# Numerators of the attention on 32x32 tiles: eight token tiles at once in place of four, a smaller DMA scratch for GpSimd, and a new order of the parts

## The chip, the cores and the metric

The kernel runs on one core of a Trainium2 chip. The metric is the time of one execution on the device in microseconds, the median of several runs. The engines are TensorE (PE, with PEld for its weight loads), VectorE (DVE), ScalarE (ACT), GpSimd (POOL) and SyncE (SP), whose queue issues the DMAs.

## The reference, cut to what matters

2048 tokens of width 512, in f32. Branch A is linear attention with 32 heads of width 16, whose feature map is a pair of softmaxes per head; branch B is dense, Mish, dense; the output is x + A * silu(B).

```python
xn = _layernorm(x, axis=-1)
# A: per head, with q, k, v = parts of xn @ wqkv
phi_q = concat([softmax(q @ w_phi), softmax(-q @ w_phi)], -1)      # the same for phi_k
kv  = einsum("bhsf,bhsd->bhfd", phi_k, v)
z   = einsum("bhsf->bhf", phi_k)
num = einsum("bhqf,bhfd->bhqd", phi_q, kv)
den = einsum("bhqf,bhf->bhq", phi_q, z)[..., None] + 1e-6
s   = (num / den) @ wo
# B
h = xn @ w1 + b1
g = silu((h * tanh(softplus(h))) @ w2)
return x + s * g
```

The change is about num, the product of a token's 32 features of a head with that head's 32x16 matrix kv.

## The kernel before

The 2048 tokens are 16 tiles of 128. Nearly every large product is made of three fp32r matmuls on the parts hi and lo of its operands (mm3). The program is a list of parts, named in ORDER (line 36). N normalizes and transposes a tile of x; K, V and Q project a tile (K and Q with the softmaxes); A adds a pair of tiles to kv; z makes the sums; D (den, line 604) multiplies a Q tile by the reciprocal of its denominators and lets VectorE transpose it into a buffer; Ua and Ub (lines 639 and 642) are the two halves of the numerators of a group of tiles; O (att_out, line 655) applies wo and stores the tile in DRAM; L, P, M and R load and prepare for the FFN; Fa to Fd (fx, fz, fy) are its first product, G (y) its second; E is the end of a group of four tiles: silu, product with the stored attention, sum with x.

The order of TensorE is that of ORDER, word for word. For the other engines and SyncE's DMAs a planner (simulate, line 177) makes the order at build time: it goes through the program with estimated costs, gives each free engine the ready operation with the earliest due time, which comes from the place in ORDER of the TensorE part that needs it, and chooses the engine where two can do the operation (either, copy). The result is fixed. At run time each engine works its list in order and waits on semaphores.

A numerator half works on 32x32 tiles of TensorE. A tile is a row group b (32 partitions, which after VectorE's transposes of 32x32 blocks hold a head's 32 features of the tokens 32b to 32b + 31 of each token tile) and a column group m; 16 tiles exist at a time. For each of 4 b, 4 m, 2 s and 2 c there is one matmul with a stationary 32x32 piece of kv and 128 moving columns: 64 matmuls for a half, 128 for a group of four token tiles, two halves each for four groups. Each is f32, and the trace shows two records for it:

```python
PE.matmul(pn[b][32 * m:32 * m + 32, c, :], w["kv"][at, h % 4, h // 4 * 32:h // 4 * 32 + 32],
          ph[at, h].rearrange("p j n -> p (j n)"), start=s == 0, stop=s == 1, skip_group_check=True)
```

The moving operand is the transposed Q of a group (ph, from a pool of one buffer of 16 KB a partition, tag tq). The four results pn (one bank of PSUM each, of eight) are kept over both halves; after the second, 8 pairs of operations on ScalarE and VectorE (split, line 429) copy them out as hi and lo parts oh and ol, in four tiles from the pool "slot". The pool's 38 buffers of 4 KB also hold weights, FFN operands and prefetched loads.

Of the kernel before, what the change touches and what calls it, by code (L numbers as in the profile page):

```python
# [12 lines left out]
F32R = mybir.dt.float32r  # L13
# [19 lines left out]
SLOTS, S2 = 38, 11  # L33
SLACK, AHEAD, LAT = 15000, 40000, 150
WAKE = 13
ORDER = """
wk0 N0 wv0 b1 wq0 N1 N2 P3 wk1 K0 N4 N8 K1 wv1 V1 K2 V0 V2 N5 K4 N3 K8 V3 K3 wq1 N6 N7 K5 A0 V4 V5 N9 A1 N10 K9 K6 K7
V6 N12 P2 A2 V7 V8 P0 V9 L0 Fa3 K10 N11 A3 A4 V11 K11 Fa0 V12 K12 V10 Fb0 Fc0 N13 Fb3 Fc3 Q5 Fd3 P1 Fd0 N14 N15 A5 V15
K13 V14 K14 K15 V13 Fa1 Fb1 Fc1 P6 Fa6 M2 Fa2 A6 A7 Fb6 Fc6 Fd1 Q4 P4 Fa4 Q0 Fd6 Fb2 z D0 D4 P5 Fa5 Q1 Fb5 Fc5 Q8 Fb4
Fc4 Fd5 M4 Fc2 Fd4 Fd2 L1 Fa9 Fb9 Q2 D1 Fa11 Fb11 Fc11 M1 Q6 Fc9 Fd11 Fd9 D5 M6 Fa13 D6 D2 Q3 Fb13 Fc13 D3 Fa8 Fb8 Fc8  # L40
Fd13 Q10 Q14 Fd8 M0 Fa7 Fb7 Q9 Fc7 D8 Ua0 D9 Q7 Fd7 Ub0 M5 Fa12 wo1 Fb12 Fc12 Q11 Fd12 D7 Q15 Q12 M3 Fa10 Fb10 Fc10
wo0 O0 O1 R2 Fd10 Ua1 R5 O3 O2 R4 R0 G7 R1 G8 Ub1 G9 O7 R3 Q13 G0 G1 G2 G3 R6 G4 G5 G6 D10 O6 O5 G10 G11 G12 G13 E0 O4
E1 G14 D11 D12 D13 Ua2 G15 Ub2 G16 G17 G18 G19 G20 D14 D15 Ua3 O10 O11 O9 Ub3 G21 G22 O14 O15 O8 E2 O13 O12 G23 G24
G25 G26 E3
"""
ACT_SET = {AF.Exp: 1, AF.Silu: 3, AF.Mish: 2}

# [5 lines left out]
class Program:  # L53
# [317 lines left out]
def block_kernel(ctx: ExitStack, tc: tile.TileContext, x, wqkT, wv, phi, wo, w1, b1, w2, out):  # L371
    nc = tc.nc
    prog = Program(nc)
    PE, V, G, A, Q = (Engine(prog, e) for e in ("PE", "V", "G", "A", "Q"))
# [3 lines left out]
    psum = ctx.enter_context(tc.tile_pool(name="psum", bufs=8, space=bass.MemoryType.PSUM))  # L378
    dram = ctx.enter_context(tc.tile_pool(name="dram", bufs=1, space=bass.MemoryType.DRAM))
    pools = {}  # L380
    for tag, n in (("slot", SLOTS), ("s2", S2), ("sm", 13), ("rq", 5), ("st", 3 * NT), ("tq", 1)):
        pools[tag] = ctx.enter_context(tc.tile_pool(name=tag, bufs=n))
        prog.cap[tag] = n
    prog.cap["ps"] = 8
# [2 lines left out]
    def bank(shape, name):  # L387
        t = psum.tile(shape, F32, tag="ps", name=name)
        prog.tag[t.tensor.name] = "ps"
        return t  # L390

    def alloc(tag, shape, name, dtype=F32):
        t = pools[tag].tile(shape, dtype, tag=tag, name=name)
        prog.tag[t.tensor.name] = tag
        return t

    def slot(shape, name, dtype=F32):
        return alloc("slot", shape, name, dtype)
# [171 lines left out]
    ek, eq, rq, phT, oT = {}, {}, {}, {}, {}  # L570
# [33 lines left out]
    def den(t):  # L604
        ez = slot([P, H, 2, DH], f"ez{t}")
        either(ez, eq[t], w["z"], op=ALU.mult)
        tz = sm([P, 2 * H], f"tz{t}")
        V.tensor_reduce(tz, ez.rearrange("p h s d -> p (h s) d"), axis=X, op=ALU.add)
        r = rq.pop(t)
        dn = sm([P, H], f"den{t}")  # L610
        V.tensor_tensor(tz, tz, r, op=ALU.mult)
        tz3 = tz.rearrange("p (h s) -> p h s", s=2)
        V.scalar_tensor_tensor(dn, tz3[:, :, 0], 1e-6, tz3[:, :, 1], op0=ALU.add, op1=ALU.add)
        V.reciprocal(dn, dn)
        r3 = r.rearrange("p (h s) -> p h s", s=2)
        V.tensor_tensor(r3, r3, dn[:, :, None].to_broadcast([P, H, 2]), op=ALU.mult)
        scale(eq[t], r)

        g, j = divmod(t, 4)
        if g not in phT:  # L620
            phT[g] = alloc("tq", [P, H, 4, 32], f"ph{g}")
        V.transpose(phT[g][:, :, j, :], eq[t].rearrange("p h s d -> p h (s d)"))

    pns = {}

    def num_half(g, i):
        ph, pn = phT[g], pns[g]
        with one():
            for c in (2 * i, 2 * i + 1):
                for s in range(2):  # L630
                    for m in range(4):
                        h = 8 * c + 2 * m + s
                        for b in range(4):
                            at = slice(32 * b, 32 * b + 32)
                            PE.matmul(pn[b][32 * m:32 * m + 32, c, :], w["kv"][at, h % 4, h // 4 * 32:h // 4 * 32 + 32],
                                      ph[at, h].rearrange("p j n -> p (j n)"), start=s == 0, stop=s == 1, skip_group_check=True)
            prog.halves()

    def num_a(g):
        pns[g] = [bank([P, KC, P], f"pn{g}_{b}") for b in range(4)]  # L640
        num_half(g, 0)

    def num_b(g):
        num_half(g, 1)
        pn = pns.pop(g)
        for u in (2 * g, 2 * g + 1):
            oT[u] = slot([P, KC, 2, P], f"oh{u}", F32R), slot([P, KC, 2, P], f"ol{u}", F32R)
        for b in range(4):
            for u in range(2):
                src = pn[b].rearrange("p k (j n) -> p k j n", j=4)[:, :, 2 * u:2 * u + 2]  # L650
                split(src, *(o[:, :, :, 32 * b:32 * b + 32] for o in oT[2 * g + u]))

    sdram = [dram.tile([P, D], F32, name=f"so{t}") for t in range(NT)]

    def att_out(t):
        u, j = divmod(t, 2)
        pw = bank([P, D], f"pw{t}")
        oh, ol = oT[u]
        with one():
            for k in range(KC):  # L660
                mm3(pw, (oh[:, k, j], ol[:, k, j]), w["o"][k], k == 0, k == KC - 1)
        so = s2(f"so{t}")
        copy(so, pw)
        Q.dma_start(sdram[t], so)
# [162 lines left out]
    w = {n: [None] * KC for n in "kqvo"}  # L827
# [17 lines left out]
    def sums():  # L845
# [20 lines left out]
        for i in range(4):  # L866
# [4 lines left out]
    wkT = load_wT(KC, "wk", 0, 2) + load_wT(KC, "wk", 1, 2)  # L871
    parts = {"b1": bias, "z": sums,
             "wk": weights_k, "wv": weights_v, "wq": weights_q, "wo": weights_o, "N": norm, "K": k_proj, "V": v_proj, "A": kv_acc, "Q": q_proj, "D": den, "Ua": num_a, "Ub": num_b,
             "O": att_out, "L": load_g, "P": prep1, "M": again1, "R": prep2,
             "Fa": ffn1a, "Fb": ffn1b, "Fc": ffn1c, "Fd": ffn1d, "G": ffn2, "E": final}
    for c in ORDER.split():
# [3 lines left out]
        else:  # L880
            n = c.rstrip("0123456789")
# [31 lines left out]
```

## Time and profile before

| | |
|---|---|
| median of 3 runs | 526.24 us (525.88 to 526.98) |
| span of the profiled execution, first to last instruction | 524.5 us |
| DMA | 120.29 MB, mean 229 GB/s |
| numerators (pn), TensorE records | 1024 |
| transposes (ph), VectorE | 16 |
| copies out of pn, ScalarE and VectorE | 32 and 32 |

Of the profiled execution the span is known; what lies around it is at most the difference to the runs shown, 1.7 us to the median. [...] A group of instructions reads "engine operation out<-in partitions x elements xcount | busy us, mean ns | idle us just before <- what ended it". All operations that the planner places carry one line, L345, so that tiles are told apart by names: pn the numerators, oh and ol their parts, ph the transposed Q, wv0 and wv1 the halves of V's weights (wvr as loaded, h and l the parts), u, sr and xx the operands of E.

### The profile page before, as it was taken

The page shows a single profiled execution, that of the slowest core. Times are in us where ns is not written, and L with a number is a line of the kernel's source. Part 1 is how long each engine was busy: PE and PEld are TensorE (multiplying, and loading weights), DVE is VectorE, ACT ScalarE, POOL GpSimd, SP SyncE. Part 2 cuts the span into 40 slices and gives each one's busy share as a digit, 9 for nine tenths or more (in the row PEclk, how much of TensorE's full clock was granted, in tenths as well). Part 3 has the DMA queues.
Part 4 walks back from the last instruction along what each step waited for, and adds up shares of the span by engine and source line. Part 5 has one row for each costly group of instructions (what it writes and reads, how often), then busy time and mean ns, then how long its engine had stood idle before and what let it go on. Part 6 is the DMA issues. An engine that isn't in the chain of part 4 may idle for free.

```text
span 524.5 us, 9183 instructions
## 1 busy us (share of the span) xinstructions
PE 517.3 (99%) x3512; PEld 427.6 (82%) x3512; DVE 366.4 (70%) x514; ACT 268.8 (51%) x385; POOL 284.0 (54%) x177
## 2 busy tenths in 40 slices
PE   8999999999999999999999999999999999999996
PEld 8788887888888788878888888788888888888885
DVE  5799999979893698869989697541469759035104
ACT  5866655446453525332333578584484946367101
POOL 2789889859693654736724364130386997004000
PEclk9999999999999999999999999999999999999999
DMA  8897959736977899987896778332659327063632
GB/s 305 257 364 226 310 182 356 250 128 225 336 269 258 285 344 362 386 246 255 258 326 196 232 273 279 141 132 81 225 184 310 140 87 241 1 215 108 204 117 80
DMA packets 84554, 120.29 MB, mean 229 GB/s; under 512 B 7072, under 2 KB 49440, under 8 KB 84512
## 3 DMA queue, kind: packets, MB, share of 16 engines
q1 hardware_dynamic: 84368, 119.47, 67.1%
q8 instruction: 27, 0.44, 0.4%
q10 hardware_dynamic: 144, 0.26, 0.2%
q14 instruction: 15, 0.12, 0.1%
HBM read 71.08 MB, written 48.63 MB: 228 GB/s over the span
## 4 chain that ended last, share of the span: by engine, by line
PE 90%; DVE 6%; issue 1%; POOL 1%; ACT 1%; DVEq 0%; POOLq 0%; ACTq 0%
PE y L345 29%; PE fx L345 14%; PE pw L345 8%; PE q L345 8%; PE fy L345 7%; PE v L345 6%; PE k L345 5%; PE fz L345 3%; PE pn L345 3%; PE kvp L345 2%; DVE w1s L345 1%; PE wake L345 1%; PE pt L345 1%; DVE nb L345 1%; DVE k6e L345 1%
## 5 line engine op out<-in xcount | busy, mean ns | idle before, releaser
L345 ACT ACTIVATE r<-r,b1t 128x512 f32<-128x512 f32 x56 | 37.8, 716 | 24.5 <-DMA r<-hd 20.6
L345 PE MATMUL k<-wkh,xT 128*128 128x512 f32 x128 | 42.2, 394 | 0.0
L345 PE MATMUL q<-wqh,xq 128*128 128x512 f32 x128 | 41.8, 390 | 0.0
L345 DVE TENSOR_TENSOR u<-u,sr 128x512 f32<-128x512 f32 (+1 forms) x10 | 9.0, 902 | 37.4 <-ACT u L345 25.5
L345 PEld LDWEIGHTS q<-wqh,xq 128*128 128x128 f32 x128 | 24.0, 188 | 5.2 <-issue 0.2
L345 PEld LDWEIGHTS k<-wkh,xT 128*128 128x128 f32 x128 | 24.0, 188 | 5.0
L345 ACT ACTIVATE u<-y 128x512 f32<-128x512 f32 (+1 forms) x17 | 9.6, 573 | 33.8 <-PE y L345 33.6
L345 ACT ACT_TABLE_LOAD x19 | 24.4, 1283 | 4.1 <-DMA x<-x 3.7
L345 PE MATMUL k<-wkl,xT 128*128 128x512 f32 x64 | 25.2, 394 | 0.8 <-DVE wkl L345 0.8
L345 PE MATMUL q<-wql,xq 128*128 128x512 f32 x64 | 24.9, 389 | 0.0
L345 POOL TENSOR_TENSOR u<-u,sr 128x512 f32<-128x512 f32 x7 | 9.5, 1357 | 25.9 <-ACT u L345 25.9
L345 PE MATMUL v<-wv0h,xT 128*128 128x512 f32 x64 | 22.8, 397 | 0.0
L345 PE MATMUL v<-wv1h,xT 128*128 128x512 f32 x64 | 22.3, 390 | 0.0
L345 DVE TENSOR_REDUCE tz<-ez 128x64 f32<-128x1024 f32 x16 | 19.2, 1207 | 4.3 <-POOL ez L345 4.1
L345 ACT ACTIVATE oh<-pn 128x256 fp32r<-128x256 f32 x32 | 10.7, 386 | 17.2 <-PE pn L345 11.1
L345 DVE TENSOR_TENSOR ol<-pn,oh 128x256 fp32r<-128x256 f32 x32 | 12.0, 412 | 9.2 <-ACT oh L345 8.1
L345 DVE TENSOR_TENSOR xx<-u,xx 128x512 f32<-128x512 f32 (+1 forms) x14 | 15.7, 1128 | 3.4 <-POOL u L345 3.1
L345 ACT ACTIVATE hc<-fx 128x512 f32<-128x512 f32 x14 | 8.3, 596 | 18.3 <-PE fx L345 18.3
L345 POOL TENSOR_TENSOR rs<-rs,mhalf 128x1 f32<-128x1 f32 x16 | 10.8, 687 | 12.4 <-DVE rs L345 12.4
L345 ACT ACTIVATE x<-x,nb,rs 128x512 f32<-128x512 f32 x15 | 11.9, 810 | 9.7 <-DVE nb L345 9.7
L345 ACT ACTIVATE v<-v 128x512 f32<-128x512 f32 x16 | 9.4, 593 | 13.9 <-PE v L345 13.9
L345 POOL TENSOR_TENSOR w1sl<-w1s,w1sh 128x1024 fp32r<-128x1024 f32 x4 | 10.6, 2653 | 8.9 <-ACT w1sh L345 7.1
(808 smaller groups left out, 1795.6 us busy)
## 6 DMA issues: line engine op xcount, KB each, us to landing
r<-hd SPq DMA_DIRECT2D x28, 512.0 KB, 4.1
scr<-xT SPq DMA_DIRECT2D x16, 512.0 KB, 4.6
xq<-scr SPq DMA_DIRECT2D x16, 512.0 KB, 5.6
w1b<-w1d SPq DMA_DIRECT2D x14, 512.0 KB, 5.4
w1b<-w1d SPq DMA_DIRECT2D x14, 384.0 KB, 4.2
raw<-xr SPq DMA_DIRECT2D x16, 256.0 KB, 4.5
fr<-raw SPq DMA_DIRECT2D x8, 512.0 KB, 6.8
so<-so SPq DMA_DIRECT2D x16, 256.0 KB, 2.1
```

The costliest lines, as they stand in the source:

```text
L345: getattr(e, m)(*a, **k)
```

## The change

Three things change.

1. A group is eight token tiles in place of four (two groups in place of four). A half's matmul has 256 moving columns, and a half works on its own four banks and its own buffer: den transposes each Q tile in two pieces of 16 heads, into ph{g}_0 and ph{g}_1; the pool tq has two buffers of 16 KB in place of one. After each half its results are copied out, 8 pairs of 256 elements, in place of 8 pairs after both. The tiles oh and ol hold two chunks of four token tiles in place of four chunks of two, and att_out reads from two of them.
2. The program is built with dynamic_dma_scratch_size=1024, GpSimd's scratch for DMA descriptors in SBUF.
3. ORDER is a new list: four halves in place of eight, and nearly every part elsewhere than before.

```diff
-wk0 N0 wv0 b1 wq0 N1 N2 P3 wk1 K0 N4 N8 K1 wv1 V1 K2 V0 V2 N5 K4 N3 K8 V3 K3 wq1 N6 N7 K5 A0 V4 V5 N9 A1 N10 K9 K6 K7
...
-E1 G14 D11 D12 D13 Ua2 G15 Ub2 G16 G17 G18 G19 G20 D14 D15 Ua3 O10 O11 O9 Ub3 G21 G22 O14 O15 O8 E2 O13 O12 G23 G24
-G25 G26 E3
+wk0 N0 wv1 wq0 N2 wk1 N1 K0 K1 wv0 N5 N8 V2 K2 V1 V0 N3 N4 P3 K5 K4 V3 K3 K8 A0 V5 wq1 N7 N9 V4 N6 K7 A1 A2 K9 K6 V7
...
+Fa7 Fc13 M5 D4 Q10 Fd8 Fb7 M3 Fd13 Fa12 Fa10 Fb12 Fc12 wo0 Fc7 R0 D6 R2 Fd12 Fb10 Fd7 D7 Fc10 Ua0 Fd10 D9 R1 Q12 Ub0
+R4 R6 Q13 G0 wo1 Q15 O1 Q14 O2 R5 D15 O7 O0 Q11 R3 G2 O3 O5 O6 D13 D8 G4 O4 D14 G7 G10 G8 G5 G1 D12 G3 G11 G9 G6 G12
+G14 D10 G13 E0 G17 D11 Ua1 E1 G19 G16 G18 G15 Ub1 G20 O9 O10 O12 G21 G24 O13 G22 O8 G25 O15 O11 E2 O14 G23 G26 E3
...
-    for tag, n in (("slot", SLOTS), ("s2", S2), ("sm", 13), ("rq", 5), ("st", 3 * NT), ("tq", 1)):
+    for tag, n in (("slot", SLOTS), ("s2", S2), ("sm", 13), ("rq", 5), ("st", 3 * NT), ("tq", 2)):
...
-        g, j = divmod(t, 4)
-        if g not in phT:
-            phT[g] = alloc("tq", [P, H, 4, 32], f"ph{g}")
-        V.transpose(phT[g][:, :, j, :], eq[t].rearrange("p h s d -> p h (s d)"))
-
-    pns = {}
+        g, j = divmod(t, 8)
+        for i in range(2):
+            if (g, i) not in phT:
+                phT[g, i] = alloc("tq", [P, H // 2, 8, 32], f"ph{g}_{i}")
+            V.transpose(phT[g, i][:, :, j, :], eq[t].rearrange("p h s d -> p h (s d)")[:, 16 * i:16 * i + 16])

     def num_half(g, i):
-        ph, pn = phT[g], pns[g]
+        ph, pn = phT[g, i], [bank([P, 2, 2 * P], f"pn{g}{i}_{b}") for b in range(4)]
...
-                            PE.matmul(pn[b][32 * m:32 * m + 32, c, :], w["kv"][at, h % 4, h // 4 * 32:h // 4 * 32 + 32],
-                                      ph[at, h].rearrange("p j n -> p (j n)"), start=s == 0, stop=s == 1, skip_group_check=True)
+                            PE.matmul(pn[b][32 * m:32 * m + 32, c % 2, :], w["kv"][at, h % 4, h // 4 * 32:h // 4 * 32 + 32],
+                                      ph[at, h % 16].rearrange("p j n -> p (j n)"), start=s == 0, stop=s == 1, skip_group_check=True)
             prog.halves()
+        for u in (2 * g, 2 * g + 1):
+            oT[u, i] = slot([P, 2, 4, P], f"oh{u}{i}", F32R), slot([P, 2, 4, P], f"ol{u}{i}", F32R)
+        for b in range(4):
+            for u in range(2):
+                src = pn[b].rearrange("p k (j n) -> p k j n", j=8)[:, :, 4 * u:4 * u + 4]
+                split(src, *(o[:, :, :, 32 * b:32 * b + 32] for o in oT[2 * g + u, i]))
...
     def att_out(t):
-        u, j = divmod(t, 2)
+        u, j = divmod(t, 4)
...
-                mm3(pw, (oh[:, k, j], ol[:, k, j]), w["o"][k], k == 0, k == KC - 1)
+                oh, ol = oT[u, k // 2]
+                mm3(pw, (oh[:, k % 2, j], ol[:, k % 2, j]), w["o"][k], k == 0, k == KC - 1)
...
-    nc = _bacc.Bacc("TRN2", target_bir_lowering=False, num_devices=1)
+    nc = _bacc.Bacc("TRN2", target_bir_lowering=False, num_devices=1, dynamic_dma_scratch_size=1024)
```

What this does to the engines' lists, at three places. First TensorE, at the start of the first half Ua0: before,

```order
L345 MATMUL fx_738<-t31h,w1b_736 128x512
L345 MATMUL pn_0_757<-ph_568,kvw 32x128 [waits DVE_49]
L345 MATMUL pn_1_758<-ph_568,kvw 32x128
L345 MATMUL pn_2_759<-ph_568,kvw 32x128 [waits DVE_49]
L345 MATMUL pn_3_760<-ph_568,kvw 32x128 [waits DVE_49]
```

and of the change:

```order
L344 MATMUL fx_760<-t31h,w1b_753 128x512
L344 MATMUL pn_0_791<-ph_0_530,kvw 32x256 [waits DVE_49]
L344 MATMUL pn_1_792<-ph_0_530,kvw 32x256
L344 MATMUL pn_2_793<-ph_0_530,kvw 32x256
L344 MATMUL pn_3_794<-ph_0_530,kvw 32x256 [waits DVE_49]
```

The matmuls follow each other as before (b turns fastest), with twice the columns; there are 64 in each of the four halves.

Second VectorE, at the last Q tiles that the last group's first half needs: before, tiles 14 and 15 ahead of Ua3,

```order
L345 TENSOR_TENSOR q14r<-q14r,den_1006 128x64 [waits DVE_49]
L345 RECIPROCAL den_1009<-den_1009 128x32 [waits DVE_49]
L345 TENSOR_TENSOR q15r<-q15r,den_1009 128x64 [waits DVE_49]
L345 STREAM_TRANSPOSE ph_974<-q14e 128x32x32 [waits Pool_49]
L345 TENSOR_TENSOR q15e<-q15e,q15r 128x1024 [waits DVE_49]
L345 STREAM_TRANSPOSE ph_974<-q15e 128x32x32 [waits DVE_49]
```

and of the change, tiles 10 and 11 ahead of Ua1:

```order
L344 TENSOR_TENSOR q10e<-q10e,q10r 128x1024 [waits DVE_49]
L344 STREAM_TRANSPOSE ph_0_803<-q10e 128x16x32 [waits DVE_49]
L344 STREAM_TRANSPOSE ph_1_804<-q10e 128x16x32
L344 TENSOR_TENSOR u_0_959<-u_0_959,sr_0_958 128x512 [waits DMAHW0_49,Activation_49]
L344 TENSOR_TENSOR u_0_962<-u_0_962,sr_0_961 128x512 [waits DMAHW4_49,Activation_49]
L344 STREAM_TRANSPOSE ph_0_803<-q11e 128x16x32 [waits Pool_49]
L344 TENSOR_TENSOR xx_0_960<-u_0_962,xx_0_960 128x512 [waits DMAHW5_49,DVE_49]
L344 TENSOR_TENSOR u_0_968<-u_0_968,sr_0_967 128x512 [waits DMAHW1_49,Activation_49]
L344 STREAM_TRANSPOSE ph_1_804<-q11e 128x16x32
```

A transpose of 32 heads has become two of 16, and two products of E0, u by sr, which wait for a load and for ScalarE's Silu, now stand ahead of tile 11.

Third ScalarE, at the first V weights: before,

```order
L345 ACTIVATE wkh_186<-wkf_189 128x512 [waits PE_49]
L345 ACTIVATE x_196<-x_196,nb_201,rs_199 128x512 [waits DMAHW1_49,DVE_49]
L345 ACTIVATE x_204<-x_204,nb_209,rs_207 128x512 [waits DMAHW2_49,DVE_49]
L345 ACTIVATE wv0h<-wvr_152 128x1024 [waits DMAHW3_49]
L345 ACTIVATE w1ah_178<-w1a_176 128x768 [waits DMAHW4_49]
L345 ACTIVATE wv1h<-wvr_218 128x1024 [waits DMAHW5_49]
```

and of the change:

```order
L344 ACTIVATE wkh_168<-wkf_171 128x512 [waits PE_49]
L344 ACTIVATE xT_176<-pt_178 128x512 [waits PE_49]
L344 ACTIVATE xr_179<-pt_178 128x512 [waits DMAHW3_49]
L344 ACTIVATE wv0h<-wvr_192 128x1024 [waits DMAHW3_49]
L344 ACTIVATE x_195<-x_195,nb_200,rs_198 128x512 [waits DMAHW1_49,DVE_49]
L344 ACTIVATE wv1h<-wvr_152 128x1024 [waits DMAHW4_49]
```

The first half of V's weights is now ahead of both normalizations x that wait for VectorE, and the second is behind one of them.

More of the change, by code (lines that the diff above doesn't have):

```diff
@@ L36 @@
 ORDER = """
-wk0 N0 wv0 b1 wq0 N1 N2 P3 wk1 K0 N4 N8 K1 wv1 V1 K2 V0 V2 N5 K4 N3 K8 V3 K3 wq1 N6 N7 K5 A0 V4 V5 N9 A1 N10 K9 K6 K7
[L38 to L42, printed above, removed]
-E1 G14 D11 D12 D13 Ua2 G15 Ub2 G16 G17 G18 G19 G20 D14 D15 Ua3 O10 O11 O9 Ub3 G21 G22 O14 O15 O8 E2 O13 O12 G23 G24
-G25 G26 E3
+wk0 N0 wv1 wq0 N2 wk1 N1 K0 K1 wv0 N5 N8 V2 K2 V1 V0 N3 N4 P3 K5 K4 V3 K3 K8 A0 V5 wq1 N7 N9 V4 N6 K7 A1 A2 K9 K6 V7
+V8 N11 V9 V6 P2 P0 K11 N10 N12 L0 A4 A3 V11 V12 Fa3 K10 V10 K12 Fa0 Fb0 Fb3 Fc0 Fc3 Fd0 N15 A5 Fd3 V15 N14 N13 K15 K13
+P1 P6 K14 Fa1 Fb1 V14 Fa6 V13 Fc1 A6 A7 M2 Fb6 z Q0 D0 Fd1 P4 Fc6 Q3 Fa4 Fd6 b1 Q2 P5 Fa5 Q9 Q1 Fb4 Q5 D2 Q8 Fa2 Fc4
+Fb2 Fb5 Fc5 Fc2 Fd5 D1 Fd2 Q7 L1 Fa9 Fb9 M4 Fc9 Fa11 M1 Fd4 Fa8 D5 Fb11 Fc11 Fd9 Fb8 D3 Fc8 Q6 M6 Fd11 M0 Fa13 Q4 Fb13
+Fa7 Fc13 M5 D4 Q10 Fd8 Fb7 M3 Fd13 Fa12 Fa10 Fb12 Fc12 wo0 Fc7 R0 D6 R2 Fd12 Fb10 Fd7 D7 Fc10 Ua0 Fd10 D9 R1 Q12 Ub0
+R4 R6 Q13 G0 wo1 Q15 O1 Q14 O2 R5 D15 O7 O0 Q11 R3 G2 O3 O5 O6 D13 D8 G4 O4 D14 G7 G10 G8 G5 G1 D12 G3 G11 G9 G6 G12
+G14 D10 G13 E0 G17 D11 Ua1 E1 G19 G16 G18 G15 Ub1 G20 O9 O10 O12 G21 G24 O13 G22 O8 G25 O15 O11 E2 O14 G23 G26 E3
 """
@@ L634, in num_half @@
                             at = slice(32 * b, 32 * b + 32)
-                            PE.matmul(pn[b][32 * m:32 * m + 32, c, :], w["kv"][at, h % 4, h // 4 * 32:h // 4 * 32 + 32],
-                                      ph[at, h].rearrange("p j n -> p (j n)"), start=s == 0, stop=s == 1, skip_group_check=True)
+                            PE.matmul(pn[b][32 * m:32 * m + 32, c % 2, :], w["kv"][at, h % 4, h // 4 * 32:h // 4 * 32 + 32],
+                                      ph[at, h % 16].rearrange("p j n -> p (j n)"), start=s == 0, stop=s == 1, skip_group_check=True)
             prog.halves()
+        for u in (2 * g, 2 * g + 1):
[4 more added lines that the diff above has]
+                split(src, *(o[:, :, :, 32 * b:32 * b + 32] for o in oT[2 * g + u, i]))
     def num_a(g):
-        pns[g] = [bank([P, KC, P], f"pn{g}_{b}") for b in range(4)]
         num_half(g, 0)
@@ L644, in num_b @@
         num_half(g, 1)
[L645 to L651, printed above, removed]
     sdram = [dram.tile([P, D], F32, name=f"so{t}") for t in range(NT)]
     def att_out(t):
-        u, j = divmod(t, 2)
+        u, j = divmod(t, 4)
         pw = bank([P, D], f"pw{t}")
-        oh, ol = oT[u]
         with one():
             for k in range(KC):
-                mm3(pw, (oh[:, k, j], ol[:, k, j]), w["o"][k], k == 0, k == KC - 1)
+                oh, ol = oT[u, k // 2]
+                mm3(pw, (oh[:, k % 2, j], ol[:, k % 2, j]), w["o"][k], k == 0, k == KC - 1)
         so = s2(f"so{t}")
```

## The prediction

> **What bounds the kernel now.** I read the page first: busy shares, TensorE's granted clock, the chain that ended last.
>
> ```profile
> PE 517.3 (99%) x3512; PEld 427.6 (82%) x3512; DVE 366.4 (70%) x514; ACT 268.8 (51%) x385; POOL 284.0 (54%) x177
> ...
> PEclk9999999999999999999999999999999999999999
> ...
> PE 90%; DVE 6%; issue 1%; POOL 1%; ACT 1%; DVEq 0%; POOLq 0%; ACTq 0%
> ```
>
> TensorE is busy 517.3 of 524.5 us at full clock and makes 90% of the chain. So what counts is TensorE time taken out, plus or minus places where TensorE waits. Next comes the chain in order of time around the first two numerator halves (columns: start us, length us, what).
>
> ```profile
> 270.48 1.36 PE fx L345 x6
> 271.84 1.83 PE pn L345 x103
> 273.67 2.94 PE q L345 x12
> ...
> 279.33 1.83 PE pn L345 x96
> 281.16 1.58 PE fx L345 x6
> ...
> 288.20 2.72 PE q L345 x12
> ```
>
> A numerator half (pn, 64 matmuls in the program, two records each) takes 1.83 us, and the group right behind it is 0.22 us longer than elsewhere (q 2.94 against 2.72, fx 1.58 against 1.36): changing tile shape costs that much. One half is worth 1.83 + 0.22 = 2.05 us, and the eight of them 16.4 us.
>
> The early stage is the other place that matters: SyncE's timeline, the DMA issues (last column: us to landing), ScalarE's timeline, and the chain, 5 to 24 us.
>
> ```profile
> 5.71 0.65 SPq L345 DMA_DIRECT2D wvr<-wv  x1
> ...
> wvr<-wv SPq DMA_DIRECT2D x2, 512.0 KB, 7.4
> ...
> 16.04 1.52 ACT L345 ACTIVATE x<-x,nb,rs 128x512 f32<-128x512 f32 x2 [0.67 <-DVE nb L345]
> 17.47 1.06 ACT L345 ACTIVATE wv0h<-wvr 128x1024 fp32r<-128x1024 f32 x1
> ...
> 15.99 2.58 issue
> ...
> 18.60 2.41 POOL wv0l L345
> 21.01 2.37 POOL wv1l L345
> ...
> 23.42 1.42 PE v L345 x5
> ```
>
> TensorE's first V projection stood until 23.42 for the low parts of wv on GpSimd. These waited for the high part on ScalarE (17.47), which stood behind two normalizations that waited for VectorE; its load was due at about 5.71 + 7.4 = 13.1.
>
> **The change, part by part.** *Numerators.* Eight halves of 64 matmuls with 128 columns become four halves of 64 with 256. The trace has no 32x32 matmul with 256 columns, so its price is bounded from both sides. Three views carry it: pn's records by stretch of the first half (PE's bracket counts matmuls under way, PEld's the weight loads), the groups by shape (busy us, mean ns), and the chain's first 128-column matmuls on the whole array.
>
> ```profile
> 271.77:272.01 0.24, 0.24 (x32) 0.24 (x33) 0.00 (x0) 0.00 (x0) 1.00 1.15 461
> 272.01:272.19 0.18, 0.18 (x33) 0.10 (x1) 0.00 (x0) 0.00 (x0) 1.00 1.01 410
> 272.19:272.63 0.44, 0.44 (x48) 0.42 (x34) 0.00 (x0) 0.00 (x0) 1.00 1.04 428
> 272.63:273.06 0.43, 0.43 (x56) 0.42 (x34) 0.00 (x0) 0.00 (x0) 1.00 0.92 363
> ...
> L345 PE MATMUL pn<-ph,kvw 32*32 32x128 f32 x1024 | 15.2, 278 | 0.0
> ...
> 6.24 1.79 PE wkf L345 x16
> ```
>
> One f32 record of 128 columns (wkf, whole array) takes 1.79/16 = 0.112 us; a 256-column record has 0.112 us more to stream.
> - Lower end: the added columns are hidden. The half stays at 1.83: 4 x 2.05 = 8.2, so 8.2 us go.
> - Upper end: a half takes twice its time: 4 x (3.66 + 0.22) = 15.5, so only 0.9 us go.
>
> In the first 0.24 us, 32 matmuls and 33 loads start: all 16 tiles with both records, 7.5 ns a pair. Then one load in 0.18 us, then a beat of 34 loads in each 0.43 to 0.44 us. The mean over a half is 1.83/128 = 14.3 ns a pair, so issue can go nearly twice as fast as the beat does, and the beat is not set by issue alone. Within a beat a tile streams only 2 x 0.112 = 0.224 us; the rest looks like the latency of a record (mean 0.278 us, of which 0.112 is streaming). If that fixed part stays, each beat gets two passes longer, and a half, whose tiles take four matmuls of two records each, gets 8 x 0.112 = 0.90 us longer: 2.73 us. Then 4 x (2.73 + 0.22) = 11.8, and 4.6 us go. I take this, near the middle, because the beat shows tiles that stream half of the time: neither full nor free.
>
> [...]
>
> *VectorE's transposes and the evacuation.* (Tile view, duration min/median/max; page, groups.)
>
> ```profile
> L345 DVE STREAM_TRANSPOSE ph<-q0e x1: 1231/1231/1231, 194.5 to 194.5; 128x1024 f32<-128x1024 f32 x1
> ...
> L345 DVE STREAM_TRANSPOSE ph<-q15e x1: 1245/1245/1245, 444.1 to 444.1; 128x1024 f32<-128x1024 f32 x1
> ...
> L345 ACT ACTIVATE oh<-pn 128x256 fp32r<-128x256 f32 x32 | 10.7, 386 | 17.2 <-PE pn L345 11.1
> L345 DVE TENSOR_TENSOR ol<-pn,oh 128x256 fp32r<-128x256 f32 x32 | 12.0, 412 | 9.2 <-ACT oh L345 8.1
> ```
>
> Sixteen transposes of about 1.24 us become 32 of half the data: between nothing more (proportional) and 16 x 1.24 = 19.8 us more on VectorE (each as long as before). I take near nothing; VectorE's 158 free us hide it, and without that cover the numerators would come later by what is added to eight tiles, up to 10 us. The evacuation keeps its 32 + 32 pieces of 256 elements, but eight of each now also come between the first and second half. They need 8 x 0.386 = 3.1 us on ScalarE and 8 x 0.412 = 3.3 us on VectorE; TensorE has Fd10 and Q12 there, 2.72 + 2.72 = 5.4 us. Four numerator banks, two of the FFN and one of Q are seven of eight, so the second half needs three back; covered by 2 us. After Ub1 the first att_out, O9, needs all eight pieces, with G20 (24 matmuls, 5.49 us by the row of 120 below) as cover. Cost nothing; without cover, up to 3.3 us at each place.
>
> *The wait for the transposed buffers.*
>
> ```profile
> DVE ph L345 <- PE pn L345: 4.3, 2, 3.1
> ```
>
> VectorE waited twice, 4.3 us in all, until a half had read the one buffer. Now each half has its own, but g = 1 needs both back: q9e's second transpose waits for Ub0, and behind it in VectorE's queue stand the evacuation's pieces of Ub0, which couldn't run sooner, and Q12's and Q13's softmax, for which no TensorE part stands close. I take nothing; the ends are nothing and one more wait of 3.1 us, on VectorE.
>
> *The new order, early.* ScalarE now makes wv0h ahead of the next normalizations (its rows in the section on the change). The second load of wv also stands right behind the first on SyncE's queue, with w1's and b1's loads moved later. ScalarE would reach wv0h at 17.47 - 1.43 - 0.67 = 15.4 (without the two normalizations and the wait), so the low parts can be ready 2.1 us earlier. TensorE gains between nothing (K's low parts or the transposes of x are then late) and 2.1 us; I take 1.0.
>
> *The new order, elsewhere.* The chain names one further wait of TensorE before 92 us:
>
> ```profile
> 85.87 1.83 DVE nb L345
> 87.71 0.02 issue
> 87.73 0.82 ACT x L345
> 88.56 0.04 issue
> 88.60 0.66 PE pt L345 x4
> ```
>
> At 88 us TensorE stood for ScalarE's x, this for nb in VectorE's queue: under 0.9 us. It may go or come back elsewhere; I take nothing, with ends -0.9 and +3 us (three such places more). The DMAs of the moved steps keep their number, all on SyncE's queue; the eight tiles of a group's attention live until its second half is used up, which may hold up loads of other parts, and that is in the +3. The last E3 stands behind the same last part G26, so the end keeps its length.
>
> *The DMA scratch.*
>
> ```profile
> q1 hardware_dynamic: 84368, 119.47, 67.1%
> ```
>
> Of 120.29 MB, 119.47 go through the queue that SyncE feeds, and no row of the issues names GpSimd. The scratch costs and gains nothing; it pays in SBUF for the second buffer.
>
> **Sum.** Span 524.5 - 4.6 - 1.0 = 518.9. The median of the three runs shown, 526.24, is 1.74 above that span, so 520.6 us.
>
> **The rivals.**
>
> *Free columns.* If issue sets the beat after all, the half stays at 1.83 and 8.2 us go: 526.24 - 8.2 - 1.0 = 517.0. For it: 64 matmuls of two records fit the mean of 14.3 ns just as well. Against: 7.5 ns a pair in the first stretch.
>
> *Doubled halves.* If the tiles of one row group take turns, a half takes 3.66 us and 0.9 go: 526.24 - 0.9 - 1.0 = 524.3. For it: 16 tiles at 0.112 us a record, all at once, would need 8 x 0.112 = 0.9 us for a half, and 1.83 is twice that. Against: 33 loads and 32 matmuls start within 0.24 us. [...]
>
> *New waits eat the gain.* The order was redone whole; three or so waits of the size at 88 us give back 3 us: 523.6.
>
> *The last tile comes late (slower).* In the new order VectorE must pass two of E0's products (u by sr) and more before it transposes q11e, the last tile that the half Ua1 needs. E0 needs the Silu behind G6. Between G6 and Ua1 TensorE has four parts (G12, G14, G13, G17) of 24 matmuls:
>
> ```profile
> 428.41 27.44 PE y L345 x120
> ...
> DVE u L345 <- ACT u L345: 25.5, 6, 17.0
> ...
> DVE u L345 <- DMA sr<-so: 11.9, 2, 11.1
> ```
>
> 27.44/120 x 24 = 5.49, four of them 22.0 us of cover. The longest waits seen for these two, 17.0 and 11.1, make 28.1, and all of them 37.4. The kernel gets slower once the way to q11e exceeds 22.0 + 5.6 + 1.1 = 28.7 us; halfway between 28.1 and 37.4 (32.8) TensorE stands 10.8 us and the time is 526.24 - 5.6 + 10.8 = 531.4. Against: these waits lie mostly at the kernel's end, where the work itself is late.
>
> **How the numbers follow.** Forecast 0.60, with an own range of 519.0 to 522.5; free columns 0.12; doubled halves 0.11; new waits 0.10; late tiles 0.07. A measurement of this kernel can tell about 0.2% (1.05 us) from no change, so faster means below 525.2. Nearly all of the first two cases lie there, and most of the third and fourth: 0.59 + 0.12 + 0.08 + 0.08 = 0.87; the rest of them is the same, 0.06; slower 0.07. The range takes in both ends of the numerators' price: from the free columns, 517.0, to the doubled halves without the early gain, 525.3; it leaves out the late tile and the tails of the others, some 0.13.
>
> **What would show it.** In the changed profile pn must have 512 records, and four pieces of the chain near 2.7 us: 1.8 says free columns, 3.7 says turns. The first v must start its second half before 23.4 us. VectorE's transposes should be 32 of about 0.65 us. Ahead of the third half (g = 1, first) TensorE must not stand for VectorE; and the 0.2 us behind a half should appear four times. The forecast is wrong if new idle time of TensorE beyond 2 us shows anywhere between 25 us and the end.

## The result

| | before | changed |
|---|---|---|
| median | 526.45 us (525.88 to 526.98, 4 runs) | 518.58 us (517.88 to 519.47, 4 runs) |
| ratio | | 0.985, 95% interval 0.9834 to 0.9865 |
| span of the profiled execution | 524.5 us | 516.4 us |

The change makes the kernel 7.9 us faster; the spans differ by 8.1 us. The prediction was 520.6 us, so 2.0 us more went than its sum had: the time lies 0.4 us below the forecast's own range (519.0 to 522.5) and inside the range over both ends (517.0 to 525.3).

The page of the changed kernel, busy shares, granted clock and the engines' shares of the chain:

```profile
PE 510.5 (99%) x3000; PEld 423.4 (82%) x3000; DVE 378.4 (73%) x535; ACT 271.8 (53%) x385; POOL 268.4 (52%) x176
...
PEclk9999999999999999999999999999999999999999
...
PE 97%; ACT 1%; DVE 1%; issue 0%; ACTq 0%
```

TensorE is still busy 99% at full clock, with 512 matmul records fewer. Its share of the chain has risen from 90% to 97%, and VectorE's has fallen from 6% to 1%: TensorE waits for others less than before.

The numerators: two rows of the tile view of ph (min/median/max ns, first and last start), pn's records by stretch of the first half (TensorE's matmuls, then its weight loads, in brackets their number), and the chain around it.

```profile
L344 PE MATMUL pn<-ph,kvw x512: 374/374/398, 287.8 to 445.8; 32*32 32x256 f32 x171
L344 DVE STREAM_TRANSPOSE ph<-q11e x2: 698/698/698, 398.8 to 402.2; 128x512 f32<-128x512 f32 x2
...
288.44:289.09 0.65, 0.65 (x46) 0.52 (x34) 0.00 (x0) 0.00 (x0) 1.00 1.09 361
...
287.86 2.69 PE pn L344 x116
290.55 1.58 PE fx L344 x6
...
296.22 2.69 PE pn L344 x115
298.91 2.95 PE q L344 x12
```

A half takes 2.69 us with 256 columns, and the 0.22 us behind it are there again (fx 1.58 against 1.36, q 2.95 against 2.72). A beat is still 34 loads; it takes 0.65 us in place of 0.43 to 0.44. The last transpose of tile 11, the last tile that the third half needs, starts at 402.2 us and takes 0.70, so it ends some 16 us ahead of that half (418.8 us).

The early stage: chain, GpSimd's timeline, and what TensorE waited for there, first in the kernel before, then in the changed one (us in all, times, longest):

```profile
16.99 2.36 DVE nb L344
...
20.90 2.76 PE v L344 x12
...
16.92 2.40 POOL L344 TENSOR_TENSOR wv0l<-wvr,wv0h 128x1024 fp32r<-128x1024 f32 x1
```

```profile
PE k L345 <- DVE wkl L345: 0.8, 1, 0.8
...
PE v L345 <- POOL wv1l L345: 0.2, 1, 0.2
```

```profile
PE pt L344 <- ACT x L344: 0.5, 1, 0.5
PE k L344 <- DVE rs L344: 0.2, 1, 0.2
```

GpSimd starts on wv0's low part at 16.92 us (18.60 before), and the first v runs its 12 matmuls through from 20.90 us without a stand. What TensorE waits for now is the tile x, behind nb on VectorE, a 128x1 operation that took 2.35 us while GpSimd worked on wv0l; the other nb just ahead took 0.15 us. But the wait that shrank most is another one than the first V projection's: in the kernel before, once its real work had begun, TensorE stood longest in K0, for wkl, the low part of K's weights on VectorE, and for wv1l only 0.2 us.

### The profile page after: what moved, and what is told of

It is laid out like the page before. It is cut to its first block, busy times and chain, and to the rows that moved or that the text cites. A ratio compares the mean times of both kernels' runs of the same rounds, so it can differ in the third digit from the quotient of the medians.

```text
span 516.4 us, 8190 instructions
## 1 busy us (share of the span) xinstructions
PE 510.5 (99%) x3000; PEld 423.4 (82%) x3000; DVE 378.4 (73%) x535; ACT 271.8 (53%) x385; POOL 268.4 (52%) x176
## 4 chain that ended last, share of the span: by engine, by line
PE 97%; ACT 1%; DVE 1%; issue 0%; ACTq 0%
PE y L344 30%; PE fx L344 15%; PE v L344 9%; PE q L344 8%; PE pw L344 8%; PE k L344 7%; PE fy L344 7%; PE fz L344 4%; PE kvp L344 3%; PE pn L344 2%; PE pt L344 1%; PE wake L344 1%; DVE nb L344 0%; ACT x L344 0%; PE wkf L344 0%; PE wqf L344 0%
## 5 line engine op out<-in xcount | busy, mean ns | idle before, releaser
L344 DVE TENSOR_TENSOR u<-u,sr 128x512 f32<-128x512 f32 (+1 forms) x14 | 12.5, 902 | 36.6 <-DMA sr<-so 24.4
L344 ACT ACTIVATE so<-pw 128x512 f32<-128x512 f32 x11 | 6.6, 598 | 30.9 <-PE pw L344 30.9
L344 DVE TENSOR_REDUCE tz<-ez 128x64 f32<-128x1024 f32 x16 | 19.3, 1210 | 0.2
L344 ACT ACTIVATE u<-y 128x512 f32<-128x512 f32 (+1 forms) x17 | 9.7, 573 | 17.3 <-PE y L344 16.1
L344 ACT ACTIVATE hb<-fx 128x512 f32<-128x512 f32 x13 | 7.8, 598 | 19.0 <-PE fx L344 19.0
L344 ACT ACTIVATE ha<-fx 128x512 f32<-128x512 f32 x13 | 7.8, 596 | 14.9 <-PE fx L344 14.9
```

Source lines behind the costliest of these rows:

```text
L344: getattr(e, m)(*a, **k)
```

## Where the 8.1 us are in the two traces

I added up TensorE's time from the start of one matmul to the start of the next, and took off what the same kind of pair takes undisturbed (0.227 us for the 512-column matmul, for example). What is left over is a stand; the last row is the rest (kvp is the product that A adds up, done in bursts of 16 short matmuls a tile):

```
                                     before   changed   difference
numerators, with the change of shape                      -4.7 us
stands up to 24 us                     2.9      1.5       -1.4 us
stand at 88 us (for x)                 0.69     0         -0.7 us
stand at 223 us (for hb)               0.46     0         -0.5 us
small stands, one kvp burst fewer, start                  -0.8 us
all                                   519.1    510.9      -8.1 us
```

The stand at 223 us is seen in the chain of the kernel before, and the same place and that of the stand at 88 us in the chain of the changed one (start, length, what; ha, hb and hc are copies of fx's results):

```profile
221.47 1.23 DVE ph L345
222.71 0.57 DVE ha L345
223.28 0.61 DVE hb L345
...
223.94 1.66 PE fx L345 x6
```

```profile
222.59 1.36 PE fx L344 x6
223.94 1.36 PE fy L344 x6
...
83.18 0.87 PE pt L344 x8
84.06 3.65 PE kvp L344 x64
```

In the kernel before, a whole transpose of 1.23 us stood ahead of ha and hb in VectorE's queue, and TensorE's fx waited behind them. In the changed kernel, both places are TensorE's work alone.

## The experiments

Each ran beside the kernel before on the same chip; the ratios are to it.

**Scratch alone.** The kernel before with one argument more:

```diff
-    nc = _bacc.Bacc("TRN2", target_bir_lowering=False, num_devices=1)
+    nc = _bacc.Bacc("TRN2", target_bir_lowering=False, num_devices=1, dynamic_dma_scratch_size=1024)
```

> The kernel before with GpSimd's DMA scratch at 1 KB and nothing else. My theory: no queue that GpSimd fills carries data, so the time stays that of before, 526.4 us within 0.5. The rival: the scratch alone brings part of the gain that I didn't forecast (2 us of it), 524.5.

Measured: 526.85 us, ratio 1.0001 (0.9992 to 1.001). The scratch does nothing to the time.

**The new order with groups of four tiles**, the halves in pairs at the four places:

```diff
-Ua0 Fd10 D9 R1 Q12 Ub0
+Ua0 Ub0 Fd10 D9 R1 Q12 Ua1 Ub1
...
-D11 Ua1 E1 G19 G16 G18 G15 Ub1 G20
+D11 Ua2 Ub2 E1 G19 G16 G18 G15 Ua3 Ub3 G20
```

> The new order, the small scratch and two buffers, but the numerators of before: eight halves with 128 columns, two halves right behind each other at each of the four places, so that the changes of tile shape number four as in the change. Theory (columns are half hidden): eight halves of 1.83 against four of 2.69, 14.6 against 10.8, so 3.9 us above the change: 522.5. Rival (the gain came from the order alone): 518.6 to 519. Rival (columns are free): 518.6 + 4 x 1.83 = 525.9 would be needed, if the half with 256 had cost 1.83.

Measured: 539.03 us, ratio 1.0208 (1.0178 to 1.0238). The theory and both rivals missed by far. The chain of the profiled execution, which took 534.9 us, at the first two pairs:

```profile
287.17 3.15 PE pn L345 x176
290.31 1.92 issue
...
298.38 2.95 PE pn L345 x159
301.33 4.25 issue
...
306.96 4.98 PE q L345 x12
```

TensorE stops inside the second half of each pair, and the chain names nothing that it waits for ("issue"). Behind the longer stand, 12 matmuls of q take 4.98 us in place of 2.72, at a granted clock of 0.56 (306 to 312 us). So two halves of 128 records each right behind one another cost something that one half doesn't; the run says nothing of the order, and two more were made.

**Many small matmuls in a row, by themselves.** A small program, run once: three blocks of 256 f32 matmuls on the 16 tiles, with 128, 256 and 512 columns, between blocks of 60 dense 128x512 ones. Everything that they read was in SBUF long before.

```diff
+BLOCKS = [("a", 128, 4, 4), ("b", 256, 4, 4), ("c", 512, 4, 4)]
```

> As the one before, with three blocks of 256 f32 matmuls in a row (four halves) with 128, 256 and 512 columns, 14 us of dense matmuls ahead of each; the rest of the kernel is left out, the output is not the reference's. Theory (TensorE's instructions come at a limited rate: two halves in a row stood 1.9 and 4.3 us with nothing named): at 128 columns the block stands at intervals and takes near 20 us in place of 7.3, at 256 near 20 in place of 10.8, at 512 near 20 in place of 17.5. Rival (the stand in the mixed kernel had a cause there, a semaphore or a buffer): 7.3, 10.8 and 17.5 us without stands.

TensorE's timeline (start, length, ..., count, and in brackets the idle time ahead) and two stretches by window (the granted clock is 0.64 and 0.50):

```profile
22.79 2.33 PE L51 MATMUL pn<-ph,kvw 32*32 32x128 f32 x163
26.82 1.89 PE L51 MATMUL pn<-ph,kvw 32*32 32x128 f32 x128 [1.69 <-issue]
30.82 2.55 PE L51 MATMUL pn<-ph,kvw 32*32 32x128 f32 x128 [2.11 <-issue]
...
51.21 4.70 PE L51 MATMUL pn<-ph,kvw 32*32 32x256 f32 x231
56.33 2.74 PE L51 MATMUL pn<-ph,kvw 32*32 32x256 f32 x128 [0.42 <-issue]
...
77.70 17.14 PE L51 MATMUL pn<-ph,kvw 32*32 32x512 f32 x512
```

```profile
30.80:33.40 2.60, 2.55 (x128) 0.64 0.03 6
34.55:36.60 2.05, 2.05 (x93) 0.50 0.04 8
```

The same stands, with no other engine at work. After 163 records of 128 columns TensorE stands; then it goes on in portions of exactly 128 records, 4.0 and 3.7 us apart (26.82, 30.82, 34.55 us). With 256 columns the first stand comes after 231 records and is 0.42 us; with 512 columns there is none, at 17.14/512 = 33 ns a record. Read as a supply, that is some 30 ns for a record with its weight load (4.0/128 = 31 ns, 3.73/128 = 29 ns), while the 128-column ones run at 14 ns (2.33/163), and a stock of 80 to 90 records at the start (163 - 2.33/0.031 = 88; 231 - 4.70/0.031 = 79); both are estimates from these rows. A half of 128 records ran without a stand (1.83 us), two in a row stood 1.8 to 4.3 us.

The profile pages of the kernel before and of the changed one have a queue of instructions (packets, MB, share):

```profile
q8 instruction: 27, 0.44, 0.4%
...
q8 instruction: 23, 0.38, 0.3%
```

The changed kernel has 512 matmul records and 512 weight loads less, and four packets less: 256 instructions, or 128 matmuls with their loads, in a packet of some 16 KB (0.44 MB/27). By this TensorE's 3512 matmuls and 3512 loads before make 27.4 packets, and the 2056 of each in the program with twelve blocks below make 16.1, where its page has 16; so I take the queue to be TensorE's. A portion of 128 records with their loads is as many instructions as one packet. That TensorE stands for its next packet is my estimate from these counts; no run shows it, nor why the stand of 4.25 us is the longest.

**The price of a column, by itself.** Blocks of 64 f32 matmuls (128 records) between dense ones, with 64 to 512 columns on 16 tiles, then 128 and 256 columns on fewer tiles:

```diff
+BLOCKS = [("a", 64, 4, 4), ("b", 128, 4, 4), ("c", 192, 4, 4), ("d", 256, 4, 4), ("e", 384, 4, 4), ("f", 512, 4, 4),
+          ("g", 128, 2, 4), ("h", 256, 2, 4), ("i", 128, 1, 4), ("j", 256, 1, 4), ("k", 256, 4, 2), ("l", 256, 4, 1)]
```

> Only the numerators' matmuls, on data of x: the rest of the kernel is left out, the output is not the reference's. Twelve blocks of 64 f32 matmuls in the kernel's order, with dense 128x512 matmuls between them: 64, 128, 192, 256, 384, 512 columns on all 16 tiles; 128 and 256 columns on 8 tiles (two column groups) and on 4 (one column group); 256 columns on two row groups and on one. Theory (a fixed latency in each beat, plus the streaming of two passes): on 16 tiles a block grows by 8 x 0.107 us per 128 columns: 1.83 at 128, 2.26 at 192, 2.69 at 256, 3.5 at 384, 4.4 at 512, and at 128 columns half of the tiles take hardly longer (2.0 us, a tile then streams most of the time). Rival (issue): flat at 1.83 up to 256, and the same on 8 and 4 tiles. Rival (tiles of a row group take turns): proportional to the columns, 3.66 at 256, and one row group with four column groups takes longer than four row groups with one column group.

TensorE's timeline, the blocks b and d on 16 tiles, g and h on 8, i and j on 4:

```profile
30.27 1.90 PE L52 MATMUL pn<-ph,kvw 32*32 32x128 f32 x128
52.95 2.76 PE L52 MATMUL pn<-ph,kvw 32*32 32x256 f32 x128
...
91.45 2.03 PE L52 MATMUL pn<-ph,kvw 32*32 32x128 f32 x128
102.70 3.68 PE L52 MATMUL pn<-ph,kvw 32*32 32x256 f32 x128
115.62 3.70 PE L52 MATMUL pn<-ph,kvw 32*32 32x128 f32 x128
128.55 7.11 PE L52 MATMUL pn<-ph,kvw 32*32 32x256 f32 x128
```

From 128 to 256 columns a block gains 0.86 us on 16 tiles, 1.65 on 8, 3.41 on 4: doubled as the tiles are halved. So the tiles stream side by side, each its own 8, 16 or 32 records of 128 more columns (0.86/8 = 0.108 us, near the 0.112 of the prediction), and 1.04 us of a 16-tile block (1.90 - 0.86) doesn't depend on columns. On 8 and 4 tiles this part is 0.38 and 0.29 us (2.03 - 1.65, 3.70 - 3.41), so it shrinks where more records follow each other on one tile; what it consists of isn't shown. Neither free columns nor doubled halves. Of the two blocks on fewer row groups, k (two row groups, four column groups) took 3.68 us, as h did. The last, l (one row group, four column groups), took 9.24 us, longer than j as the rival of turns has it, but at a granted clock of 0.76; times that clock it is 7.0 us (an estimate), j's 7.11.

**The new order with groups of four, the halves apart.** At least 5 us of other work between any two:

```diff
-R4 R6 Q13 G0 wo1 Q15 O1 Q14 O2 R5 D15 O7 O0
+R4 R6 wo1 Q13 Q15 Ua1 O1 O2 Ub1 G0 Q14 O0 R5 D15 O7
...
-D11 Ua1 E1 G19 G16 G18 G15 Ub1 G20
+D11 Ua2 E1 G19 Ub2 G16 G18 Ua3 G15 Ub3 G20
```

> The new order again with eight halves of 128 columns, now each half at least 5 us of other TensorE work from the next (two projections, two att_out or two G between them). Theory: 8 x 2.05 against 4 x 2.91 us, 4.8 us above the change (0.985 of the kernel before, 519 on this scale): 523.7. Rival (the two halves side by side were slow for the tiles' sake, not for the instructions): it stays near 1.02.

Measured: 523.28 us, ratio 0.9933 (0.9921 to 0.9945). The stands inside the halves are gone; in its chain each of the last four halves is one piece of 1.83 us, as before. This run splits the gain: the new order (and the scratch) is worth (1 - 0.9933) x 526.5 = 3.5 us with the old numerators (2.9 to 4.2 by the interval), and the new numerators in it another (0.9933 - 0.985) x 526.5 = 4.4 us. The order isn't quite that of the change, since some parts moved to part the halves; so the split is as good as those moves are harmless.

**The new numerators in the old order**, three forms. In the first, the output projections O stood right behind the second half; in the second, the halves and the O's were a part further apart; in the third, the first half came one part later and the denominators of tiles 14 and 15 one earlier. The cut shows the second form against the kernel before:

```diff
-wo0 O0 O1 R2 Fd10 Ua1 R5 O3 O2 R4 R0 G7 R1 G8 Ub1 G9 O7
+wo0 R2 Fd10 Ua0 R5 R4 R0 G7 R1 G8 Ub0 G9 O0 O1 O3 O2 O7
...
-G19 G20 D14 D15 Ua3 O10 O11 O9 Ub3 G21 G22
+G19 D14 D15 Ua1 G20 Ub1 G21 O10 O11 O9 G22
```

> The new numerators in the order of before: Ua0, Ub0, Ua1, Ub1 at the places of Ua1, Ub1, Ua3, Ub3, and the seven att_out parts that came too early moved right behind them. Theory: the numerators alone bring 4 x 2.69 + 4 x 0.22 against 8 x 2.05, 4.8 us: 521.7, and TensorE's stands of before stay (2.9 us up to 24 us, 0.7 at 88 us, 0.5 at 223 us). Rival (the numerators bring it all): 518.6. Rival (the order brings it all): 526.

> The other half of a two-by-two table: the numerators of eight token tiles (256 columns, 32 transposes, two buffers, 1 KB of scratch) in the order of before, changed only so far that the four halves stand apart from each other and the output projections of a group stand at least one part behind its second half. The run of the new order with groups of four stands 3.5 us below the kernel before. Theory (the numerators give 4.7 by themselves, whatever the order): 526.5 - 4.7 = 521.8, ratio about 0.991. Rival (the gain of the numerators needs the new order, since the transposed buffers or the split pieces come late in the old one): stands of TensorE for ph or ol, and 523.5 or more, as in the first form of this run, which stood for ol by 11 us. If the two parts add up, this run's gain and that run's gain make the whole gain of about 8.1 us.

> The last form of the eight-tile numerators in the order of before. In the form before it TensorE stood 3.0 us for hc at 302 us, since VectorE had the product and the transposes of tile 7 to do ahead of it for the first half, and 4.5 us for ph at 453 us, since one part of 5.5 us less lay ahead of the third half; behind the first stand the granted clock was halved for some 7 us, another 2.6 us. Here the first half comes one part of 24 matmuls later (5.5 us more for VectorE), and the denominators of tiles 14 and 15 come one part earlier. Theory (those two stands are what the old order lacked in cover, and the numerators themselves give 4.7 us anywhere): both stands go, and the time is 532.8 - 3.0 - 2.6 - 4.5 - 0.7 = 522.0, ratio 0.991. Rival (the old order has no room on VectorE for eight tiles' products at once, wherever the half is put): a stand of over 1.5 us appears again at one of the two groups, and the time is above 526, ratio 0.998 or more; then the gains of the numerators and of the order can't be told apart by adding.

Measured: 534.06 us, ratio 1.0141 (1.0126 to 1.0156); 532.83 us, 1.0119 (1.0099 to 1.014); 535.78 us, 1.0173 (1.0157 to 1.019). All three are slower than the kernel before, where some 0.99 was expected. First what TensorE waited for in the second form (us in all, times, longest; the profiled execution took 535.79 us, the longest of six), and VectorE's timeline ahead of the wait for hc; then the wait that the third form has beside the same one for ph:

```profile
PE pn L344 <- DVE ph L344: 4.5, 1, 4.5
PE fx L344 <- DVE hc L344: 3.0, 1, 3.0
...
297.83 3.26 DVE L344 TENSOR_TENSOR q7e<-q7e,q7r 128x1024 f32<-128x1024 f32 x1
...
301.61 1.29 DVE L344 STREAM_TRANSPOSE ph<-q7e 128x512 f32<-128x512 f32 x2
```

```profile
PE pn L344 <- DVE ol L344: 1.1, 1, 1.1
```

The first form stood 6.2 us for ol in its waits (4.7 in the O's and 1.5 in the last half), not the 11 that the expectation of the second form names. A half of eight tiles needs the product and the transposes of all eight by its start, and at these places of the old order they came late. In the second form, hc waits behind tile 7 at 302 us, with the granted clock at 0.63 from 305.3 to 309.9 us (some 1.7 us by that, 4.6 x 0.37, an estimate, where the expectation of the third form has 2.6), and the third half waits for tile 15 at 453 us. Tile 7's product took 3.26 us; tile 14's took 1.22. So some 2 of those 3 us may come of a slow product and not of the number of tiles; what slowed it isn't shown, and no run separates the two. In the third form hc's wait shrinks to 0.7 us, but the second half now waits for ol, the copies of the first, and the wait for tile 15 stays: tiles 12 to 15 come one after another through products on GpSimd and VectorE up to 454 us. Three of the four halves of the second form took 2.68 to 2.69 us (at 309.9, 323.7 and 464.4 us). The third half, behind its wait, took 4.52 us in the second form and 4.53 in the third, where a record takes up to 632 ns, against 398 in the changed kernel; the mean granted clock of both profiled executions is 0.99. The second half of the third form took 6.0 us in the chain (320.92 to 326.92 us), with waits for ol inside it and a clock of 0.89 from 318 to 324 us and 0.83 from 324 to 330. So in the orders that I tried, the gain of the numerators is had with the new order only; that no old order with small edits would hold them isn't shown.

**The old start in the new order**, up to L0, in two forms; and **the new start in the kernel before**:

```diff
-wk0 N0 wv1 wq0 N2 wk1 N1 K0 K1 wv0 N5 N8 V2 K2 V1 V0 N3 N4 P3 K5 K4 V3 K3 K8 A0 V5 wq1 N7 N9 V4 N6 K7 A1 A2 K9 K6 V7
+wk0 N0 wv0 b1 wq0 N1 N2 P3 wk1 K0 N4 N8 K1 wv1 V1 K2 V0 V2 N5 K4 N3 K8 V3 K3 wq1 N6 N7 K5 A0 V4 V5 N9 A1 N10 K9 K6 K7
```

> The change with the start of ORDER as before: the parts up to L0 in the order of before (b1 among them, N11 and K11 just ahead of L0), the rest as in the change. Theory: the start is worth the difference of TensorE's stands up to 90 us, 3.6 against 1.5 us: 518.6 + 2.0 = 520.6. Rival (the start is worth nothing, the later parts bring what I didn't forecast): 518.6.

> The change with the start of before, now with N11 and K11 well apart, so that K11 needn't wait for N11. Theory: TensorE's stands up to 24 us return, 2.9 us in place of 1.5, and 0.7 at 88 us: 2.0 above the change, ratio 0.989. Rival (the first splice was slow for the start itself): 0.993 as there.

> The kernel before with the change's order of the first parts, up to L0, and its own order and numerators from there on. Theory (the start alone gives what the accounts of matmul starts show, stands of 2.9 us before and 1.5 us after up to 24 us): 526.5 - 1.4 = 525.1, ratio 0.997. Rival (the start is worth the 3.5 us by which the change with the old start was slower): 523.0, ratio 0.9935; then the stand of 1.9 us for the weight fl at 96 us in that run came of the start and not of how the parts were spliced.

Measured: 523.31 us, ratio 0.9934 (0.9921 to 0.9946), with K11 right behind N11 and a wait of 2.0 us for its xT; 522.15 us, 0.9916 (0.9899 to 0.9933), with the two apart; and 528.75 us, 1.0039 (1.0026 to 1.0052). Waits of TensorE, of the second form and of the new start in the kernel before:

```profile
PE fz L344 <- DMA fl<-scr: 0.8, 1, 0.8
PE fz L344 <- DMA fh<-scr: 0.7, 1, 0.7
```

```profile
PE fx L345 <- DVE w1al L345: 2.0, 1, 2.0
```

In all three the stands up to 24 us are those of the start that was put in: 2.9 us with the old one, 1.5 with the new. But each splice made new waits at 80 to 230 us: 1.9 us for a load at 96 us in the second form; 2.1, 1.1 and 1.0 us for VectorE's and GpSimd's products in the last, which ate the 1.4 us and more. So none of the three times came as the theories had them: the second form is 3.5 us above the change by the ratios, not 2.0, and the last is slower than the kernel before. The start is worth 1.4 us at its place, and what it's worth in the end depends on what follows.

**One part moved.** The changed kernel with K2 ahead of N8 and V2, so that 12 matmuls cover the one stand of 0.63 us that is left at 19.5 us:

```diff
-wk0 N0 wv1 wq0 N2 wk1 N1 K0 K1 wv0 N5 N8 V2 K2 V1 V0
+wk0 N0 wv1 wq0 N2 wk1 N1 K0 K1 wv0 N5 K2 N8 V2 V1 V0
```

> The change with one part moved: K2 two places forward, ahead of N8 and V2, so that TensorE has 12 matmuls of 0.227 us to do while VectorE and ScalarE finish the tile x that N8 transposes. In the change TensorE stands 0.63 us for it at 19.5 us. Theory (the stand is a wait for that tile alone, so other work put there covers it): the stand goes, 518.6 - 0.5 = 518.1, ratio to the kernel before 0.984. Rival (the end of this stretch is set by the split value weights wv0l and wv1l, which GpSimd finishes at 19.3 and 21.7 us, or by K2's own input): the stand moves to K2 or to V2 with the same length, and the time stays at 518.6 or rises by as much as 0.6.

Measured: 524.29 us, ratio 0.995 (0.9938 to 0.9962), 5.3 us worse than the change by the ratios; both theories missed. The waits of TensorE, and its windows around the longest:

```profile
PE pt L344 <- ACT x L344: 2.9, 2, 2.3
...
PE pt L344 <- DVE x L344: 0.7, 1, 0.7
...
57.60:60.50 2.90, 0.57 (x3) 0.97 1.04 314
60.60:63.60 3.00, 3.00 (x10) 0.50 0.58 175
```

The stand at 19.5 us went, and came back at N8 (0.7 us: its normalization is now VectorE's, behind K0's softmax), at 32 us (0.7 us) and at 58 us (2.3 us, with 3 us of half the clock behind it). The text moved one part; the built lists moved a lot, since the due times of all that hangs on N8, V2 and K2 changed. VectorE's list begins to differ so:

```order
-L344 BN_STATS st_204<-x_203 128x6
 L344 TENSOR_SCALAR rs_198<-mv_197 128x1
-L344 BN_AGGR mv_205<-st_204 128x2
+L344 TENSOR_TENSOR xT_164<-pt_166,xT_164 128x512
 L344 TENSOR_TENSOR wkl_169<-wkf_171,wkh_168 128x512
 L344 TENSOR_TENSOR xT_176<-pt_178,xT_176 128x512
-L344 TENSOR_SCALAR rs_206<-mv_205 128x1
```

x_203 is N8's tile: its statistics, ahead of the last wkl in the changed kernel, come later here.

## Why the prediction held, and where it was off

- **What bounds the kernel**: right. TensorE's time taken out and its stands make the whole difference.
- **The half at 2.73 us**: right, 2.69. The reasoning was right as well as the number: beats of 34 loads that get two passes of 0.112 us longer (0.43 + 0.22 = 0.65, measured 0.65), and the block by itself, 1.90 to 2.76 us. That the fixed part of a beat is a latency stays a guess. The term was -4.6 us; measured 4.4 by the ratios, 4.7 by the traces.
- **Free columns and doubled halves**: both refuted by the half and by the blocks on 16, 8 and 4 tiles. 8 tiles gain 1.65 us and 16 tiles, with the same row groups, 0.86, so the tiles of a row group don't take turns here.
- **Transposes, copies, buffers at nothing**: right in the new order. 32 transposes of 0.65 to 0.71 us, no wait of TensorE's matmuls for ph or ol. But the working gave too much of that to VectorE's free time as a sum: in the old order, with as much of it free, the same operations made TensorE wait up to 4.5 us. What covers them is where they stand.
- **The last tile late**: didn't happen; 16 us were left.
- **The new order, early, at -1.0**: -1.4, within the ends given, but mostly not for the reason given, so the number is in part luck. The prediction read the chain's row at 23.42 us as a long stand of the first V projection. Until then TensorE had K1's matmuls and the first half of V to do; it stood 0.3 us for wv1l, 0.4 us with the slower matmul behind. That much went by the mechanism of the prediction. Some 0.9 us went in the first two K projections, where the stands with the slower matmuls behind them fell from 1.5 to 0.6 us: the wait for wkl is gone, and no row of the prediction names it. The stands for tiles x changed places, 0.7 us of them to 19.5 us.
- **New waits**: the one at 19.5 us; beyond 25 us there is none over 0.2 us.
- **The new order elsewhere, at nothing, with ends -0.9 and +3**: this is the term that was mis-sized. With the early part it was -1.0 in the sum and is -3.5 by the run with groups of four. Of the stands behind 24 us, I had counted the one at 88 us as what could go (0.69, it went), and read the chain no further than 92 us for waits; the 0.46 us at 223 us and a number of small ones went too. They were to be seen in the trace, and the kernel before had 3.6 us of them behind 24 us, of which some 0.9 belong to the eight halves' ends; the changed one has 1.5.
- **The scratch at nothing**: right, 1.0001.
- **The sum**: right for the numerators by 0.2 us; the order's 2.5 us more are the miss, and the difference of the median to the profiled span, 2.2 us in place of 1.74, takes 0.4 back.

Open: why the new order has fewer stands, place by place, can't be read from one edit at a time, since each edit to the list reorders the other engines for hundreds of us.

## What to carry to other kernels

For work on small tiles of TensorE, add its beats: here 128 more columns cost each of 16 tiles 0.108 us a record, and 1.04 us of a block of 1.90 us didn't depend on columns: a part that fewer, wider matmuls save. And count the records that follow each other: here 512 in a row of 128 columns stood after the first 163, for 1.2 to 2.1 us at a time. A row of the chain says where it passes, not that the engine stood there: ask the engine's own waits before pricing one. Before pricing a new order, add up all the stands that the old one has over the whole span: that is the most a better order can bring, and here it was the term that I left out. An order that a planner fills in at build time is one piece; parts of it, spliced, measure the splice.

## What the runs showed of the hardware that I had not expected

- **Short matmuls in a row**: 128-column records on 32x32 tiles run at 14 ns for the first 163 in the small program and the first 233 and 208 in the first two pairs. Then come stands, of 1.2 to 2.1 us between portions of 128 in the small program, 4.0 and 3.7 us from portion to portion, and of 1.8 to 4.3 us in the pairs. At 33 ns a record (512 columns) there are none.
- **The clock behind a stand**: stands of 1.92 us (groups of four in pairs, 290 us) and 2.0 us (the new start in the kernel before, 96 us) left the granted clock at 1.00; another of 2.0 us (the old start, first form, 82 us) and one of 2.3 us (K2 moved, 58 us) were followed by 0.50 for 2 and 3 us, and those of 2.11 and 1.18 us in the small program by 0.64 and 0.50. So the length alone doesn't decide here, and 3 us at half clock add another 1.5 us (an estimate). The clock also fell inside block l of the program with twelve blocks (0.76 from 157.9 to 166.9 us), with no stand ahead.
- **A small operation on VectorE**: nb, 128x1, took 2.35 us in the changed kernel while GpSimd worked on wv0l, and 0.15 us just before; it ended with GpSimd's operation, at 19.3 us. The nb at 85.8 us in the kernel before took 1.90 us and ended with GpSimd's operation too, at 87.7 us. That VectorE waited for GpSimd is the plain reading; no run tests it.
